# Fewer idle products before the experts, and the expert probabilities moved into the first expert

## The chip, the cores and the metric

The kernel runs on one core of a Trainium2 chip. The metric is the device time of one execution in microseconds (us). The engines of the core work side by side, each through its own list of instructions in order: TensorE (PE in the rows; its weight loads are PEld), VectorE (DVE), ScalarE (ACT), GpSimd (POOL) and SyncE (SP, which here mainly starts transfers). They wait for each other by semaphores.

## The reference

Three stages follow each other, on 2 x 768 tokens of 384 numbers (8 heads of 48):

```python
# 1 attention: a state that is updated token by token
y[:, :, t] = np.einsum('bhd,bhde->bhe', q[:, :, t], state)
v_old = np.einsum('bhde,bhd->bhe', state, kt)
state = state + bt[:, :, :, None] * np.einsum('bhd,bhe->bhde', kt, vt - v_old)
# 2 experts: one of 8 for each token, kept from the token before if local_gate >= 0.5
fresh_e = int(np.argmax(logits[b, s]))
e = fresh_e if s == 0 or local_gate[b, s] < 0.5 else (prev_e if prev_e >= 0 else fresh_e)
p = np.exp(logits[b, s] - logits[b, s].max()); p /= p.sum() + 1e-09
out[b, s] = p[e] * (np.maximum(x[b, s] @ w1[e], 0.0) @ w2[e])
# 3 mixing: FFT over tokens and features, a norm, and one more MLP
u = x + mixed
ch = np.maximum(un @ w_ch1, 0.0) @ w_ch2
out = u + ch
```

Each expert has weights of 384 x 1024 and 1024 x 384. The probability `p[e]` scales an expert's output, so it is needed only when the first expert's output is written; which expert a token goes to is needed before the first product.

## The kernel before

**Stages.** Attention ends at about 240 us of the profiled execution, the routing at about 257, the experts at about 390; the mixing takes the rest. Attention is ordered by a planner (not touched here). From the routing on, the order on each engine is that of the code, with one exception: between the routing and the experts stands a branch (L989, L990) for tokens that overflow an expert's 240 slots. With these inputs its body is not entered, but all five engines read the flag and go past it. When the program is built, an instruction written behind the branch may be put ahead of it where nothing that it needs is made in between.

**Routing** (`route`, L734 to L812) turns the logits `lg` into lists. On VectorE a chain of small instructions (from `mx`, L750) finds each token's expert (`e`, as one-hot `Ot`), its rank among the expert's tokens (`rank`), and one-hots of the slot (`oh`, L801). Twelve products on TensorE (`st`) then give the list of token numbers per slot. Behind them stand the idle products: `warm(s.WARMR)`, L806, multiplies a constant by itself into the PSUM tile `wp` (L746) 20 times, and nothing reads it. In the trace each appears as two instructions. From `st` VectorE makes the gather's indices `gm` and the overflow flag `fl`. GpSimd then gathers expert 0's tokens into `xg` (L901, two indirect transfers) and, behind the branch, expert 1's. The logits minus their maximum are kept in `ls`.

**Weights.** Each expert has 4 weight pairs (a block of w1 and one of w2), 32 in all, loaded by SP into six buffers `raw` (`wload`, L855, two transfers a pair). Each number is split into a high and a low fp16 part: `whi` (L891) makes the high part on ScalarE, `wlo` (L894) the low part on VectorE from `raw` and the high part. `wlo(q)` also issues the loads of pair q+6. `whi(0)` and `whi(1)` are called ahead of the routing, `whi(2)` and `whi(3)` behind it.

**Experts** (`moe_main`, L943). First come `chosen` (L817 to L829: one exponential on ScalarE, L820, then 11 VectorE instructions that make the probability `pr` and its three fp16 parts `pp`), `wlo(0)`, and the transposes of expert 0's tokens: `xtr` transposes a third of the features on TensorE (`xtp`, L907), ScalarE copies the high part (L908), VectorE makes the low part (L909). For expert 0 the three thirds have three buffers; for later experts the tile `t` has one. Then, for each weight pair q: `h` makes 18 products (`hp`, L918), ScalarE the high part of their relu (`hh`, L920), VectorE the low part (`hl`, L921); a third of the next expert's tokens is transposed; `o` makes 12 products with the pair before (`op`, L930). In expert 0 there is more: `parts` (L813 to L816) multiplies `pp` into the one-hots, part 1 at pair 1, parts 2 and 3 at pair 2, and `slots_p` (L830 to L836) makes, at pair 3, the probability of each slot with 12 products that read `oh` and the result of `parts` (L834). Its PSUM tile is `t` too, the one buffer that the transposes use.

Of the kernel before, what the change touches and what calls it, by code (L numbers as in the profile page):

```python
# [728 lines left out]
class Rest:  # L729
    def __init__(s,tc,I,O,K,xd,x2d):  # L730
        s.tc,s.nc,s.I,s.O,s.K,s.xd,s.x2d=tc,tc.nc,I,O,K,xd,x2d

    WARMR=20
    def route(s,keep,pool,ps,lg):  # L734

        nc,K=s.nc,s.K; V,G=nc.vector,nc.gpsimd
# [8 lines left out]
        def warm(n):  # L745
            for _ in range(n): nc.tensor.matmul(out=wp,lhsT=K["ident"],rhs=K["ident"],start=True,stop=True)  # L746
# [58 lines left out]
        for j in range(12): nc.tensor.matmul(out=st,lhsT=oh[:,j],rhs=s.Wr[:,0,:,j],start=(j==0),stop=(j==11))  # L805
        warm(s.WARMR)  # L806
        s.gi=s.gidx(keep,st.rearrange("p h e -> p (h e)"),16,"m")
# [134 lines left out]
        s.scattered.append(i)  # L942
    def moe_main(s):  # L943
        dec=s.decoding(); s.sc=[]; s.scattered=[]; last=None
        s.chosen()
        s.wlo(0)
        for k in range(3): s.xtr(0,k,"h",3)
        s.wlo(1)
        next(dec)
        for q in range(32):  # L950
            e,g=divmod(q,4)
            if g==0 and e<7: s.gather(e+1)
            x=s.h(q)
            if g and e<7: s.xtr(e+1,g-1)
            s.whi(q+4)
            if last: s.o(q-1,last)
            last=x
            if q==0: s.wlo(2)
            s.wlo(q+3)
            if q==1: s.parts(1)  # L960
            if q==2: s.parts(2); s.parts(3)
            if q==3: s.slots_p()
            if g==1:
                while s.sc: s.scatter()
            if q==26: s.tables(0)
            if q==29: s.tables(1)
            if q>2:
                for _ in range(1+(g==0)): next(dec,None)
        for t in range(2):
            s.o(31,last,(t,))  # L970
            while s.sc: s.scatter()
        p=s.ps.tile([128,2,256],F32,tag="h",name="wp",bufs=3)
        for _ in range(s.WARMM): s.nc.tensor.matmul(out=p[:,0,0:128],lhsT=s.K["ident"],rhs=s.K["ident"],start=True,stop=True)

        z=s.wk.tile([128,2],F32,name="z")
        s.nc.gpsimd.memset(z[:,0:1],0.0)
        s.nc.vector.tensor_copy(out=z[:,1:2],in_=z[:,0:1])
        for _ in dec: pass
        s.wlo(35)
        for q in (36,37):  # L980
            s.whi(q); s.wlo(q)
# [546 lines left out]
```

## Time and profile before

| | |
|---|---|
| median of 3 runs | 582.86 us (581.4 to 585.84) |
| profiled execution | 580.74 us, of which the span of the trace 578.9 us |
| granted TensorE clock, mean over the span | 0.909 |
| TensorE busy | 470.7 us (81% of the span), 5162 instructions |
| VectorE busy | 421.7 us (73%), 943 |
| ScalarE busy | 322.8 us (56%), 729 |
| GpSimd busy | 78.9 us (14%), 85 |

The trace is of one execution, and its times are microseconds from the start of its span. A share of busy time is a mean over stages that have different limits, so the rows below are read by stretch: what each engine does there, and for whom it waits. The clock stands as a fraction of full speed: 1.00 is the level of 2.4 GHz, 0.50 that of 1.2 GHz.

### The profile page before, as it was taken

Reading aid. Unit: us, or ns where it says so; the run is one execution under the profiler, and the core shown is the slowest. Engines: PE = TensorE matmul, PEld = TensorE weight load, DVE = VectorE, ACT = ScalarE, POOL = GpSimd, SP = SyncE. Lnnn points to the kernel's source line nnn. Section 1 sums busy time; section 2 is a strip of 40 time slices with the busy share of each in tenths; the row PEclk is TensorE's granted clock in tenths of the full one; section 3 lists DMA queues with packets and bytes.
Section 4 is the critical chain, followed back from the end, with each engine's and each line's share of the span. In section 5 each row is a group of like instructions: output and inputs, shape, how many; then the busy total and the mean of one; then the engine's idle time right before and its main releaser. Section 6 shows DMA issues by size and latency. Waiting matters only on the chain.

```text
span 578.9 us, 12899 instructions
## 1 busy us (share of the span) xinstructions
PE 470.7 (81%) x5162; PEld 375.0 (65%) x5162; DVE 421.7 (73%) x943; ACT 322.8 (56%) x729; POOL 78.9 (14%) x85
## 2 busy tenths in 40 slices
PE   0642027894689799679999999999899999999997
PEld 0531017783689698568888888788787655555575
DVE  7969989898998877469888979878987643231132
ACT  3664347898698888716766766672554332111111
POOL 6000000000000000040343332125111210000010
PEclk9965556999599789879999999999999999999999
DMA  7274125186005103839999997328100000010011
GB/s 250 50 130 121 37 49 63 63 141 156 1 3 103 29 3 100 299 99 336 388 319 316 361 305 238 118 63 274 56 1 1 28 2 0 1 55 0 1 42 41
DMA packets 66991, 67.23 MB, mean 116 GB/s; under 512 B 40086, under 2 KB 59483, under 8 KB 66928
## 3 DMA queue, kind: packets, MB, share of 16 engines
q1 hardware_dynamic: 63936, 57.59, 33.5%
q0 software_dynamic: 2992, 8.79, 4.9%
q8 instruction: 41, 0.67, 0.5%
q14 instruction: 22, 0.18, 0.1%
HBM read 51.95 MB, written 7.67 MB: 103 GB/s over the span
## 4 chain that ended last, share of the span: by engine, by line
PE 27%; issue 18%; POOL 5%; DVE 3%; DMA 1%; ACT 1%; POOLq 0%; SPq 0%; ACTq 0%; DVEq 0%
PE mp L1373 12%; PE mop L1399 12%; POOL xg L901 3%; POOL x2d L939 2%; PE fp L1239 1%; PE yp L1208 1%; DMA xa<-x2d 1%; PE up L1320 1%; DVE zl L1192 0%; DMA x2d<-ot,sim 0%; ACT zh L1190 0%; DVE e L1127 0%; DVE Y L1265 0%; DVE ws L894 0%; DVE d L1127 0%
## 5 line engine op out<-in xcount | busy, mean ns | idle before, releaser
L1383 DVE SCALAR_TENSOR_TENSOR ml<-mp,mh 128x256 f16<-128x256 f32 (+1 forms) x48 | 26.8, 558 | 81.0 <-ACT mh L1381 80.9
L1373 PE MATMUL mp<-uT,ws 128*128 128x256 f16 (+1 forms) x432 | 77.8, 326 | 0.0
L1399 PE MATMUL mop<-ws,mh 128*128 128x384 f16 x288 | 77.7, 326 | 0.0
L1381 ACT ACTIVATE mh<-mp 128x256 f16<-128x256 f32 (+1 forms) x48 | 23.5, 489 | 89.8 <-PE mp L1373 89.6
L930 PE MATMUL op<-ws,hh 128*128 128x384 f16 (+1 forms) x256 | 67.5, 326 | 0.0
L918 PE MATMUL hp<-xT,ws 128*128 128x240 f16 x576 | 64.6, 266 | 0.9 <-DVE xT L909 0.5
L312 PEld LDWEIGHTS <-KT 128*128 128x128 f16 x576 | 27.5, 118 | 51.6 <-issue 40.1
L918 PEld LDWEIGHTS <-ws 128*128 128x128 f16 x576 | 56.2, 98 | 6.9 <-issue 1.3
L1373 PEld LDWEIGHTS <-ws 128*128 128x128 f16 x432 | 42.2, 98 | 27.2
L894 DVE SCALAR_TENSOR_TENSOR ws<-raw,ws 128x1536 f16<-128x1536 f32 x32 | 55.9, 1749 | 0.0
L312 PE MATMUL ga<-ST,KT 128*128 128x64 f16 x288 | 16.2, 224 | 42.2 <-DVE ST L308 37.7
L891 ACT ACTIVATE ws<-raw 128x1536 f16<-128x1536 f32 x32 | 47.3, 1485 | 0.7 <-DMA raw<-moe_w 0.7
L1399 PE MATMUL mop<-ws,ml 128*128 128x384 f16 x144 | 46.9, 326 | 0.0
L930 PE MATMUL op<-ws,hl 128*112 128x384 f16 (+1 forms) x128 | 41.7, 326 | 0.0
L1399 PEld LDWEIGHTS <-mh 128*128 128x128 f16 x288 | 28.2, 98 | 17.8
L901 POOL DMA_INDIRECT xg<-xd,gm x16 | 23.0, 1437 | 117.4 <-DVE fl L1063 110.0
L930 PEld LDWEIGHTS <-hh 128*128 128x128 f16 (+1 forms) x256 | 29.1, 114 | 11.6
L373 DVE TENSOR_TENSOR P<-P,tmp 128x31 f32<-128x31 f32 (+15 forms) x93 | 31.5, 338 | 1.7
L371 DVE TENSOR_TENSOR tmp<-Gu,P 128x31 f32<-128x31 f32 (+15 forms) x93 | 31.2, 336 | 1.6
L921 DVE SCALAR_TENSOR_TENSOR hl<-hp,hh 128x480 f16<-128x480 f32 x32 | 20.9, 654 | 14.5 <-ACT hh L920 12.9
L939 POOL DMA_INDIRECT x2d<-ot,sim x16 | 19.3, 1204 | 86.9 <-ACT ot L935 84.4
L920 ACT ACTIVATE hh<-hp 128x480 f16<-128x480 f32 x32 | 18.1, 567 | 20.7 <-PE hp L918 19.5
(274 smaller groups left out, 1176.9 us busy)
## 6 DMA issues: line engine op xcount, KB each, us to landing
raw<-moe_w SPq DMA_DIRECT2D x64, 384.0 KB
x<-moe_w_ch SPq DMA_DIRECT2D x24, 384.0 KB
qp<-q SPq DMA_DIRECT2D x5, 512.0 KB
kp<-k SPq DMA_DIRECT2D x6, 384.0 KB
vp<-v SPq DMA_DIRECT2D x6, 384.0 KB
xd<-yb SPq DMA_DIRECT2D x48, 48.0 KB
xa<-x2d SPq DMA_DIRECT2D x6, 384.0 KB
ur<-x2d SPq DMA_DIRECT2D x2, 768.0 KB
```

The costliest lines, as they stand in the source:

```text
L312: s.nc.tensor.matmul(out=out,lhsT=st[l],rhs=mv[m],start=(first and i==0),stop=True,skip_group_check=True)
L371: nc.vector.tensor_tensor(out=x,in0=Gu[:,k,k+1:32].unsqueeze(2).to_broadcast([128,m,n]),in1=P[:,k,0:n].unsqueeze(1).to_broadcast([128,m,n] ...
L373: nc.vector.tensor_tensor(out=P[:,k+1:32,0:n],in0=P[:,k+1:32,0:n],in1=x,op=ALU.subtract)
L891: s.nc.scalar.activation(out=s.W[q][:,0].rearrange("p s c -> p (s c)"),in_=s.raw[q],func=AF.Copy,scale=WS)
L894: s.nc.vector.scalar_tensor_tensor(out=W[1],in0=s.raw[q],scalar=WS,in1=W[0],op0=ALU.mult,op1=ALU.subtract)
L901: nc.gpsimd.indirect_dma_start(out=s.xg[e][t][0:w],out_offset=None,in_=s.xd,in_offset=bass.IndirectOffsetOnAxis(ap=s.gi[0:w,8*t+e:8*t+e+1] ...
L918: nc.tensor.matmul(out=p[:,i],lhsT=s.W[q][:,a,i,128*k:128*k+128],rhs=xT[b][:,k],start=(n==0),stop=(n==8)); n+=1
L930: nc.tensor.matmul(out=s.po[t][0:w],lhsT=hs[a][:,i,128*t:128*t+w],rhs=s.W[q][:,b,i,384:768],start=(g==0 and i==0 and n==0),stop=(g==3 and ...
L939: i=s.nc.gpsimd.indirect_dma_start(out=s.x2d,out_offset=bass.IndirectOffsetOnAxis(ap=s.si[0:w,c:c+1],axis=0),in_=ot,in_offset=None,bounds_ ...
L1373: for k in range(3): nc.tensor.matmul(out=p,lhsT=s.w_ch1(a,k,f),rhs=s.uT[g][b][:,k,0:N],start=(n==0),stop=(n==8)); n+=1
L1383: nc.vector.scalar_tensor_tensor(out=hl,in0=p,scalar=0.0,in1=hh,op0=ALU.max,op1=ALU.subtract)
L1399: nc.tensor.matmul(out=pm[t],lhsT=hs[a][:,128*t:128*t+128],rhs=s.w_ch2(b,f),start=(f==0 and n==0),stop=(f==11 and n==2))
```

## The change

There are three edits. The number of idle products goes from 20 to 13. `chosen()` is no longer called at the head of `moe_main`, so that `wlo(0)` is the first call there. And `chosen()` is called at weight pair 1 instead, just ahead of `parts(1)`. (The overflow branch has a call of its own to `chosen`, which stays.) Behind L945 the lines of the changed kernel have numbers that are lower by one.

```diff
-    WARMR=20
+    WARMR=13
     def route(s,keep,pool,ps,lg):
...
         dec=s.decoding(); s.sc=[]; s.scattered=[]; last=None
-        s.chosen()
         s.wlo(0)
         for k in range(3): s.xtr(0,k,"h",3)
...
             s.wlo(q+3)
-            if q==1: s.parts(1)
+            if q==1: s.chosen(); s.parts(1)
             if q==2: s.parts(2); s.parts(3)
             if q==3: s.slots_p()
```

On VectorE, at the start of the routing (the copies of the logits `lg` end attention, `mx` begins the routing), the built program differs by one row:

```order
L540 SCALAR_TENSOR_TENSOR U_116<-ups,U_113 64x96 x2
L643 COPY lg<-eps 32x9 x3
+L894 SCALAR_TENSOR_TENSOR ws<-raw,ws 128x1536
L750 TENSOR_REDUCE mx<-lg 128x12
L752 SCALAR_TENSOR_TENSOR rf<-lg,rc 128x12
```

The low part of weight pair 0 is still written behind the branch, where `chosen` stood ahead of it, but with `chosen` gone it is built ahead of the whole routing.

SyncE's list at the same place, with the last writes of attention's output (`xd`), the overflow flag (`fl`), and the weights' loads (`raw`), before:

```order
L855 DMA raw<-moe_w 128x2x384 x12
L160 DMA xd<-yb 32x4x96 x8
L989 TENSOR_LOAD fl
```

and after:

```order
L855 DMA raw<-moe_w 128x2x384 x12
L160 DMA xd<-yb 32x4x96 x8
L855 DMA raw<-moe_w 128x2x384 x2
L988 TENSOR_LOAD fl
```

The two loads of pair 6, which `wlo(0)` issues, moved with it to the place ahead of the flag.

On ScalarE, the first instructions behind the branch, with the semaphores for which each waits in brackets (`ex` is the exponential in `chosen`, `xT` the transposed tokens of expert 0), before:

```order
L820 ACT_TABLE_LOAD [waits DVE_49]
L820 ACTIVATE ex<-ls 128x96 [waits Activation_49]
L908 ACTIVATE xT<-xtp 128x240 [waits DVE_49,DMASW6_49,PE_49,Activation_49]
L908 ACTIVATE xT<-xtp 128x240 [waits PE_49] x2
L920 ACTIVATE hh<-hp 128x480 [waits PE_49]
```

and after:

```order
L908 ACT_TABLE_LOAD [waits DVE_49,DMASW6_49,PE_49]
L908 ACTIVATE xT<-xtp 128x240 [waits Activation_49]
L908 ACTIVATE xT<-xtp 128x240 [waits PE_49] x2
L920 ACTIVATE hh<-hp 128x480 [waits PE_49]
L891 ACTIVATE ws<-raw 128x1536 [waits DMAHW7_49,DMAHW6_49,Pool_49]
L920 ACTIVATE hh<-hp 128x480 [waits PE_49]
L908 ACTIVATE xT<-xtp 128x240 [waits PE_49]
L891 ACTIVATE ws<-raw 128x1536 [waits DMAHW1_49,DMAHW0_49]
L820 ACTIVATE ex<-ls 128x96
```

The table load now belongs to the first copy of transposed tokens, and stands behind that copy's wait for TensorE; the exponential follows eight rows later.

On VectorE in expert 0, from the low part made at pair 1 on, before:

```order
L894 SCALAR_TENSOR_TENSOR ws<-raw,ws 128x1536
L815 TENSOR_TENSOR ph<-pp,hi 128x24
L816 TENSOR_TENSOR W<-Ot,ph 128x96 x2
L921 SCALAR_TENSOR_TENSOR hl<-hp,hh 128x480
L909 SCALAR_TENSOR_TENSOR xT<-xtp,xT 128x240
```

and after, down to the first row of `parts`:

```order
L894 SCALAR_TENSOR_TENSOR ws<-raw,ws 128x1536
L821 TENSOR_REDUCE se<-ex 128x12
L822 TENSOR_TENSOR t_4385<-Ot,ex 128x96
L823 TENSOR_SCALAR se<-se 128x12
L824 TENSOR_REDUCE pr<-t_4385 128x12
L825 RECIPROCAL se<-se 128x12
L826 TENSOR_TENSOR pr<-pr,se 128x12
L828 CAST pp<-pr 128x12
L829 TENSOR_TENSOR pr<-pr,pp 128x12
L828 CAST pp<-pr 128x12
L829 TENSOR_TENSOR pr<-pr,pp 128x12
L828 CAST pp<-pr 128x12
```

The eleven instructions of `chosen` stand between the low part and `parts(1)`; the rows behind them are the same as before.

## Rows read from the trace of the kernel before

**Rows 1.** Windows by stage: busy time of each engine, clock, DMA share, GB/s:

```profile
core 0: us, PE busy (x) PEld busy (x) DVE busy (x) ACT busy (x) POOL busy (x), PEclk, DMA share, GB/s
240.80:249.70 8.90, 2.45 (x28) 1.69 (x29) 6.95 (x31) 4.50 (x4) 0.00 (x0) 0.51 0.41 133
249.70:256.80 7.10, 7.04 (x43) 6.85 (x43) 3.83 (x17) 1.57 (x2) 3.86 (x4) 0.66 0.39 108
262.60:272.90 10.30, 10.30 (x82) 8.30 (x80) 10.20 (x20) 6.44 (x9) 0.00 (x0) 1.00 1.00 354
272.90:390.00 117.10, 116.88 (x940) 97.34 (x939) 100.30 (x116) 79.70 (x106) 36.60 (x29) 1.00 0.78 267
```

**Rows 2.** Grouped lines, TensorE, 262.6 to 390 us: busy, mean ns, idle before:

```profile
L918 PE MATMUL hp<-xT,ws 128*128 128x240 f16 x543 | 61.0, 266 | 0.2
```

**Rows 3.** Timeline, start of the routing: start, us, engine, line, operation [idle before]:

```profile
239.70 1.48 ACT L891 ACTIVATE ws<-raw 128x1536 f16<-128x1536 f32 x1
...
240.61 0.17 DVE L643 COPY lg<-eps 32x9 f32<-32x9 f32 x1 [0.61 <-PE eps L637]
240.82 0.25 DVE L750 TENSOR_REDUCE mx<-lg 128x12 f32<-128x96 f32 x1
```

**Rows 4.** Timeline from the idle products to the first transposes:

```profile
249.75 6.99 PE L746 MATMUL wp<-ca 128*128 128x128 f32 x40
...
250.39 1.03 POOL L901 DMA_INDIRECT xg<-xd,gm  x1 [110.04 <-DVE fl L1063]
...
251.72 0.94 POOL L901 DMA_INDIRECT xg<-xd,gm  x1 [0.30 <-POOLq L990]
251.82 1.28 ACT L820 ACT_TABLE_LOAD   x1 [6.52 <-DVEq L990]
...
253.12 0.28 ACT L820 ACTIVATE ex<-ls 128x96 f32<-128x96 f32 x1
253.43 0.25 DVE L821 TENSOR_REDUCE se<-ex 128x12 f32<-128x96 f32 x1 [2.77 <-issue]
...
254.22 0.94 POOL L901 DMA_INDIRECT xg<-xd,gm  x1 [0.30 <-DMA xg<-xd,gm]
...
255.48 1.76 DVE L894 SCALAR_TENSOR_TENSOR ws<-raw,ws 128x1536 f16<-128x1536 f32 x1
257.22 0.62 PEld L907 LDWEIGHTS xtp<-ca,xg 128*128 128x128 f32 x6 [0.67 <-PEq L990]
257.25 0.82 PE L907 MATMUL xtp<-ca,xg 128*128 128x128 f32 x6 [0.51 <-DVE ws L894]
```

**Rows 5.** DMA issues, 253.5 to 255 us: the gather's, and us to landing:

```profile
xg<-xd,gm POOLq DMA_INDIRECT x2, 3.1
```

**Rows 6.** Timeline, expert 0: TensorE and the ScalarE row used:

```profile
264.81 2.01 PE L918 MATMUL hp<-xT,ws 128*128 128x240 f16 x18
...
266.86 0.57 ACT L920 ACTIVATE hh<-hp 128x480 f16<-128x480 f32 x1 [1.80 <-PE hp L918]
...
268.81 2.01 PE L918 MATMUL hp<-xT,ws 128*128 128x240 f16 x18
...
272.90 0.46 PE L834 MATMUL sp<-W,oh 128*128 128x48 f16 x12
...
273.20 0.47 PE L918 MATMUL hp<-xT,ws 128*128 128x240 f16 x3
```

**Rows 7.** Timeline, expert 0: VectorE:

```profile
266.03 1.75 DVE L894 SCALAR_TENSOR_TENSOR ws<-raw,ws 128x1536 f16<-128x1536 f32 x1
...
267.70 0.17 DVE L815 TENSOR_TENSOR ph<-pp,hi 128x24 f16<-128x24 f16 x1
...
268.24 0.65 DVE L921 SCALAR_TENSOR_TENSOR hl<-hp,hh 128x480 f16<-128x480 f32 x1
...
272.44 0.40 DVE L909 SCALAR_TENSOR_TENSOR xT<-xtp,xT 128x240 f16<-128x240 f32 x1
```

**Rows 8.** Windows of half a microsecond around the clock's rise:

```profile
254.50:255.00 0.50, 0.50 (x6) 0.50 (x5) 0.42 (x3) 0.00 (x0) 0.50 (x1) 0.96 0.71 138
```

## The prediction

> **What bounds the kernel now.** I read the windows by stage first [rows 1]. From 262.6 us to 390 us TensorE is busy for 10.30 of 10.30 us and 116.88 of 117.10 us: the experts are bound by it, and the grouped lines put only 0.2 us of idle time before its products there [rows 2]. So a delay at the experts' first product, or a stall inside expert 0, reaches the end of the kernel in full. The 18 us ahead of that (240.8 to 258.6) are the routing: a chain of small VectorE instructions, with TensorE busy for 2.45 of 8.90 us and then only with idle products. This stretch is all that the change touches, with expert 0.
>
> The timeline of the routing's start [rows 3] shows VectorE copying the last logits at 240.61 and starting the routing's first reduction at 240.82, with no gap. ScalarE begins the first of four high parts at 239.70 and needs 1.48 us for it.
>
> The timeline from the idle products to the first expert [rows 4] shows three things. The idle products run from 249.75 for 6.99 us, to 256.74; the first transposes follow at 257.25, 0.51 us later. The gather's data are there earlier: the first gather starts at 250.39, and the fourth, which waits for its landing, starts at 254.22, 3.8 us after; the second starts at 251.72 and lands 3.1 us (the fourth gather's landing time, [rows 5]) to 3.8 us later, at 254.8 to 255.5. And the probabilities (table load at 251.82, VectorE from 253.43) and weight pair 0's low part (255.48 to 257.24) run beside the idle products. All this is covered by the idle products, and the transposes wait for their end alone: the row names the low part (its end, 257.24) as what released them, but their weight load began at 257.22, before it.
>
> In expert 0, VectorE is busy for 10.20 of 10.30 us [rows 1]. TensorE there moves in lockstep: one product group starts at 264.81 and the next at 268.81, 4.00 us; the one after starts at 273.20, 4.39 us later [rows 6]. Between them are the 12 slot products, 0.30 us (272.90 to 273.20), so 0.09 us was waiting. What they waited for is VectorE: its third low part of the next expert's tokens runs 272.44 to 272.84 [rows 7], reads the PSUM tile `t` of which there is one buffer, and the slot products need that buffer; they start at 272.90. VectorE's slack there is nothing.
>
> **The change, part by part.** *The low part of pair 0 moves, and further than its line says.* The order of the built program puts it, with its two weight loads on SP's queue, ahead of the routing's first reduction. It needs the high part, done at 239.70 + 1.48 = 241.2, and takes 1.76 us [rows 4]: to 242.9. The reduction, at 240.82 before, starts 2.1 us later, and with it the whole routing, the idle products (251.85), the gathers and the branch: all on VectorE's chain or behind it. SP's two loads stand behind the last writes of attention and in front of SP's read of the overflow flag; they wait for 242.9, the flag is due at 252. Their 0.79 MB fall into the routing, whose DMA share is 0.41 [rows 1], and cost nothing; were they late, they would meet the gathers at 252.5.
>
> *13 idle products in place of 20.* Each is two instructions, so 26 in place of 40. TensorE's clock stood at half (0.51 on the mean, the 1.2 GHz level) through the routing [rows 1] and rose to full by 254.5, 4.8 us after the first idle product (0.96 in 254.5 to 255.0) [rows 8]. With 4.75 us at half and 2.24 us at full clock for 40, one takes (4.75 + 2 x 2.24) / 40 = 0.23 us at half and 0.115 at full. If the clock rises at the same moment, 254.5, 2.65 us at half clock do 11.5 of the 26 and the other 14.5 take 1.67 us: the end is 256.2. If it rises only 4.8 us after the later start, at 256.65, 20.9 are done by then and the end is 257.25. So the end lies between 256.2 and 257.3 (256.74 before), and the transposes could start at 256.7 to 257.8. The second gather lands at 254.8 + 2.1 = 256.9 at the earliest, 257.6 at the latest. The pair of transposes for the first third ends at about 257.25 with the early bounds (before: 257.25 + 0.4 = 257.65), a gain of 0.4 us; with the late ones at 258.2, a loss of 0.55. I take the early bounds, because the fourth gather belongs to the same burst and the clock's rise is read at 254.5: **-0.4 us** (range -0.4 to +0.55). The 7 products that go pay for 2.1 us of later routing, and no more.
>
> *ScalarE's table load.* Before, the first ScalarE instruction behind the branch was the exponential, so its table load, 1.28 us at 251.82, lay beside the idle products. In the built order the load now stands at the copy of the first transposed tokens, and the wait for TensorE stands on the load, not behind it. ScalarE takes its instructions in order, so the load starts when the transposes end: **+1.28 us** on the path to the first product. It costs nothing only if it could be run ahead of its wait, and the exponential at 253.12, 0.01 us behind the load's end, shows nothing more than 1.28 either: bounds 0 and 1.28, and I take the row. The Trainium skill (ScalarE: Activation LUTs, What ACT_TABLE_LOAD costs) gives 1283 ns for the load and some 1380 ns of drain more. The trace agrees on the first and shows no drain, ScalarE having stood idle before; an estimate from the page's two figures makes the sum 4.3 us, not 2.9.
>
> *The probabilities go into expert 0.* Eleven small VectorE instructions ran from 253.43 until the low part started at 255.48: **2.05 us**. They now stand behind the low part of 266.03 and in front of the part at 267.70 [rows 7]. Everything behind them on VectorE, up to the tokens' low part that ends at 272.84, has no gap, so it comes 2.05 us later, and TensorE's slot products with it: +2.05 in full. Bounds: 0, if VectorE could catch up; 2.05 by the rows. The exponential (0.28) goes into ScalarE's idle 1.80 us ahead of 266.86 [rows 6] and costs nothing. Behind the slot products both engines are late by the same amount.
>
> **Sum:** -0.4 + 1.28 + 2.05 = +2.9 us. The profiled execution took 580.74 us (span 578.9), so 583.7 for it. The three timed runs have their median at 582.86, 2.1 us above the profiled one, and spread from 581.4 to 585.84; on that median the forecast is 582.86 + 2.9 = 585.8 us, 0.5% slower. About 1% is what a measurement of this kernel can tell from no change, so this lies within it.
>
> **Rivals.** *The late bounds hold* (clock and landing): +0.55 in place of -0.4, +3.9 us, 586.8. For it speaks that nothing ties the clock's rise to a time in the program; against it, the 254.5 in the rows. Chance 0.17.
>
> *The table load is hidden*: -0.4 + 2.05 = +1.65, 584.5. Against it stands the order of the waits. Chance 0.10. *It costs twice its row*, a wait as long again behind it: +1.28 more, 587.1. The exponential began 0.01 us behind the load's end, so 0.03. The Trainium skill (ScalarE: Activation LUTs, What ACT_TABLE_LOAD costs) names such a wait.
>
> *Not slower: VectorE catches up in expert 0.* If the slot products do not wait, as they would not with 2.05 us of idle time on VectorE ahead of 272.4, the sum is +0.9, 583.7, no difference. It decides at slack 2.05 us; the rows show 0.1. Chance 0.10. Coming out over 1% faster would need this, a hidden load and more.
>
> *Slower by over 1%: the idle products end before the clock rises*, and it stays at half into expert 0. Twenty products rose it after 4.8 us; 13 last 26 x 0.23 = 6.0 us at half clock, so 1.2 us decide. If it fails, the transposes start at 251.85 + 6.0 + 0.5 = 258.35, 1.1 later than before, and the first 4.8 us of expert products run at half speed and lose 2.4: 1.1 + 0.2 (transposes) + 1.28 + 2.4 + 2.05 = +7.0, 589.9. Chance 0.06. The Trainium skill (TensorE: Matmul & The Clock Gate, What's actually happening) says that the slow state is the default and activity lifts it; by that, the cut idle products are the risk of this change.
>
> *The weights arrive earlier.* Pair 6's load starts some 13 us sooner; but products waited 0.2 us in all behind 262.6 [rows 2], so at most 0.2 is gained, and it is left out.
>
> **How the numbers follow.** Forecast with its own terms 0.50 (585.8), late bounds 0.17 (586.8), hidden load 0.10 (584.5), costlier load 0.03 (587.1), caught up 0.10 (583.7), cold clock 0.06 (589.9), anything else 0.04. The range leaves out the cold clock and takes in the others, with some of the spread of the runs: from caught up and hidden load together (582.86 - 0.4 = 582.5, and 0.5 of spread: 582.0) to the costlier load (587.1, and 1.1 of spread: 588.2). Slower than 588.7 (over 1%): the cold clock and the spread above the late bounds, 0.10. Faster than 577.0: 0.03. Within 1%: 0.87.
>
> **What would show each step.** Right: the routing's reduction near 242.9, behind a low part; a table load just behind the first transposes, with the experts' first product near 259.5 (258.60 before); the slot products near 272.90 + 0.9 + 2.05 = 275.8; TensorE without gaps behind. Wrong: a reduction still at 240.8; a load that ended before the transposes; slot products that come only as late as the first product; or a granted clock of 0.50 behind 258.

## The result, and the profile after

| | before | changed |
|---|---|---|
| median of 11 runs each | 583.06 us | 588.13 us (587.01 to 590.3) |
| ratio, 95% interval | 1 | 1.0089 (1.0072 to 1.0106) |
| profiled execution | 580.74, span 578.9 | 588.09, span 586.3 |
| mean granted clock | 0.909 | 0.895 |

The changed kernel is slower by 5.2 us (583.06 x 0.0089; 4.2 to 6.2 by the interval). The forecast was +2.9 us and 585.8; the measured 588.13 lies at the very top of its range. Direction and most of the places were right, the size was not: 2.3 us were missing.

The two spans differ by 7.4 us, more than the medians, and the first reading is why. Rows of the timeline at the start of the routing, after (start, us, engine, line, operation, idle time before):

```profile
242.68 0.17 DVE L643 COPY lg<-eps 32x9 f32<-32x9 f32 x1 [0.61 <-PE eps L637]
243.28 1.76 DVE L894 SCALAR_TENSOR_TENSOR ws<-raw,ws 128x1536 f16<-128x1536 f32 x1 [0.43 <-ACT ws L891]
244.96 0.24 DVE L750 TENSOR_REDUCE mx<-lg 128x12 f32<-128x96 f32 x1
```

Attention ended 2.07 us later in this execution (last logits at 242.68; 240.61 in [rows 3]), with nothing of the change in it. In the 17 traces of this study the last logits lie between 240.6 and 244.7, in four executions of the changed kernel alone between 242.3 and 242.7. So where times of two traces are compared below, each is counted from the last logits of its own trace. Counted so, the reduction `mx` starts at 2.28, before at 0.21: the low part ahead of the routing costs 2.07 us, as forecast (2.1).

What follows on TensorE and ScalarE up to the first product, after, in the same view (rows [rows 4] answer to these):

```profile
253.88 5.89 PE L746 MATMUL wp<-ca 128*128 128x128 f32 x26
...
260.23 0.82 PE L907 MATMUL xtp<-ca,xg 128*128 128x128 f32 x6 [0.45 <-PE wp L746]
260.70 1.28 ACT L908 ACT_TABLE_LOAD   x1 [13.33 <-PE xtp L907]
...
262.00 0.89 ACT L908 ACTIVATE xT<-xtp 128x240 f16<-128x240 f32 x3
...
262.86 5.51 PE L918 MATMUL hp<-xT,ws 128*128 128x240 f16 x36 [1.81 <-DVE xT L909]
```

The 13 idle products, 26 instructions in the trace, take 5.89 us, 0.227 us an instruction: nearly as long as the 40 instructions of before (6.99). The table load stands alone between the transposes and the copies, and TensorE waits 1.81 us behind the transposes, where it was 0.53 before. And the 36 products of the first two groups take 5.51 us; before, two rows of 19 and 17 took 2.11 and 1.92:

```profile
258.60 2.11 PE L918 MATMUL hp<-xT,ws 128*128 128x240 f16 x19 [0.53 <-DVE xT L909]
260.90 1.92 PE L918 MATMUL hp<-xT,ws 128*128 128x240 f16 x17 [0.19 <-DVE ws L894]
```

The windows say why (busy time, clock, DMA share and GB/s of a stretch): the idle products, the transposes and the wait, the first two groups, and the experts behind expert 0's stall:

```profile
core 0: us, PE busy (x) PEld busy (x) DVE busy (x) ACT busy (x) POOL busy (x), PEclk, DMA share, GB/s
253.90:259.70 5.80, 5.80 (x29) 5.58 (x28) 0.67 (x5) 0.00 (x0) 3.85 (x4) 0.50 0.38 104
260.20:262.80 2.60, 0.82 (x6) 0.69 (x7) 0.40 (x2) 2.09 (x4) 1.27 (x2) 1.00 0.13 45
262.90:268.10 5.20, 5.20 (x35) 4.29 (x35) 3.45 (x5) 1.85 (x2) 0.51 (x1) 0.67 0.57 163
...
280.80:390.00 109.20, 108.95 (x874) 90.32 (x870) 94.99 (x110) 72.38 (x98) 34.03 (x26) 1.00 0.80 269
```

The granted clock is 0.50 (1.2 GHz) through all the idle products, 1.00 (2.4 GHz) through the transposes and the wait, in which TensorE was busy for 0.82 of 2.60 us, and 0.67 on the mean over the first two groups. Before, the idle products had 0.66 on the mean [rows 1], and the same two groups had 1.00:

```profile
258.60:262.60 4.00, 3.81 (x36) 3.39 (x36) 3.60 (x5) 1.97 (x3) 2.74 (x2) 1.00 0.75 256
```

Behind 280.8 TensorE is busy for 108.95 of 109.20 us, so nothing ahead is given back there.

In expert 0, after (VectorE, and the two places where TensorE waits for it):

```profile
273.31 0.25 DVE L821 TENSOR_REDUCE se<-ex 128x12 f32<-128x96 f32 x1
...
275.20 0.17 DVE L828 CAST pp<-pr 128x12 f16<-128x12 f32 x1
275.28 0.16 DVE L815 TENSOR_TENSOR ph<-pp,hi 128x24 f16<-128x24 f16 x1
...
276.84 0.43 PE L907 MATMUL xtp<-ca,xg 128*128 128x128 f32 x2 [0.46 <-DVE xT L909]
...
280.02 0.40 DVE L909 SCALAR_TENSOR_TENSOR xT<-xtp,xT 128x240 f16<-128x240 f32 x1
...
280.48 0.46 PE L834 MATMUL sp<-W,oh 128*128 128x48 f16 x12 [1.25 <-DVE xT L909]
```

The probabilities take 1.97 us of VectorE (273.31 to 275.28). Behind them TensorE waits twice for a low part of the tokens that has to leave the one buffer `t`: 0.46 us at the third transpose, 1.25 us at the slot products. The waits of TensorE from 253 us on name the same places:

```profile
engine line waited for: us in total, times, longest us
PE hp L918 <- DVE xT L909: 1.8, 1, 1.8
PE sp L834 <- DVE xT L909: 1.3, 1, 1.3
...
PE xtp L907 <- DVE xT L909: 0.5, 1, 0.5
```

### The profile page after: what moved, and what is told of

The parts are those of the page before. It is cut to its first block, busy times and chain, and to the rows that moved or that the text cites. A ratio compares the mean times of both kernels' runs of the same rounds, so it can differ in the third digit from the quotient of the medians.

```text
span 586.3 us, 12869 instructions
## 1 busy us (share of the span) xinstructions
PE 472.8 (81%) x5148; PEld 376.2 (64%) x5148; DVE 421.7 (72%) x943; ACT 322.5 (55%) x729; POOL 77.1 (13%) x85
## 4 chain that ended last, share of the span: by engine, by line
PE 36%; issue 21%; DVE 21%; ACT 9%; DMA 7%; POOL 5%; SPq 1%; POOLq 0%; ACTq 0%; DVEq 0%
PE mp L1372 12%; PE mop L1398 12%; POOL xg L901 3%; DVE P L373 3%; DVE tmp L371 3%; DMA raw<-moe_w 2%; DMA KT<-KBl 2%; POOL x2d L939 2%; PE wps L312 2%; PE fp L1238 1%; ACT U L512 1%; DMA vp<-v 1%; PE lps L614 1%; PE yp L1207 1%; PE wp L746 1%
## 5 line engine op out<-in xcount | busy, mean ns | idle before, releaser
L918 PE MATMUL hp<-xT,ws 128*128 128x240 f16 x576 | 66.1, 270 | 2.1 <-DVE xT L909 1.8
L930 PE MATMUL op<-ws,hh 128*128 128x384 f16 (+1 forms) x256 | 67.5, 326 | 0.0
L918 PEld LDWEIGHTS <-ws 128*128 128x128 f16 x576 | 57.2, 99 | 8.5 <-issue 2.6
L930 PE MATMUL op<-ws,hl 128*112 128x384 f16 (+1 forms) x128 | 41.7, 326 | 0.0
L930 PEld LDWEIGHTS <-hh 128*128 128x128 f16 (+1 forms) x256 | 29.1, 114 | 11.6
L901 POOL DMA_INDIRECT xg<-xd,gm x16 | 20.8, 1302 | 118.2 <-DVE fl L1062 112.0
```

Source lines behind the costliest of these rows:

```text
L901: nc.gpsimd.indirect_dma_start(out=s.xg[e][t][0:w],out_offset=None,in_=s.xd,in_offset=bass.IndirectOffsetOnAxis(ap=s.gi[0:w,8*t+e:8*t+e+1] ...
L918: nc.tensor.matmul(out=p[:,i],lhsT=s.W[q][:,a,i,128*k:128*k+128],rhs=xT[b][:,k],start=(n==0),stop=(n==8)); n+=1
L930: nc.tensor.matmul(out=s.po[t][0:w],lhsT=hs[a][:,i,128*t:128*t+w],rhs=s.W[q][:,b,i,384:768],start=(g==0 and i==0 and n==0),stop=(g==3 and ...
```

## The experiments

The times of a kernel are given as its ratio to the kernel before, timed on the same chip, with the 95% interval, and in us of 583. Lines inserted in a kernel shift the numbers behind them.

**13 idle products alone.** The kernel before with one edit:

```diff
-    WARMR=20
+    WARMR=13
```

> The kernel before with 13 idle products in place of 20, and nothing else. In the changed kernel all 26 instructions of the idle products ran at half clock, 0.2265 us each. From 249.75 us on, where they start in the kernel before, that ends at 255.65 in place of 256.74, so the transposes and the experts' first product come 1.1 us earlier. Theory 1 (the clock is what 13 products cost): the clock then stands at half in part of expert 0's first two product groups, which cost 1.3 us in the changed kernel, so the time is about that of before: +0.2 us, 583.3 (from -1.1 to +0.6). Rival (the half clock there was a chance of that one execution): -1.1 us, 582.0.

Measured: 0.9989 (0.9971 to 1.0006), -0.6 us (-1.7 to +0.3). Its timeline on TensorE:

```profile
251.94 4.72 PE L746 MATMUL wp<-ca 128*128 128x128 f32 x26
257.33 0.30 PE L907 MATMUL xtp<-ca,xg 128*128 128x128 f32 x1 [0.68 <-DVE pr L829]
258.48 0.73 PE L907 MATMUL xtp<-ca,xg 112*128 112x112 f32 x5 [0.84 <-DMA xg<-xd,gm]
259.79 2.11 PE L918 MATMUL hp<-xT,ws 128*128 128x240 f16 x19 [0.58 <-ACT xT L908]
```

The same 26 instructions took 4.72 us here, 5.89 in the changed kernel: the clock rose 3.3 us after the first of them, there only behind the last. The transposes start 2.2 us earlier than before, but half of that is lost at once, since the second transpose waits 0.84 us for the second gather, issued at 253.90; the wait ends 4.6 us behind the issue. The first product comes 1.1 us earlier, at full clock. The time lies between the two expectations; it decides neither, but 13 products as such cost nothing.

**The move alone, with 20 idle products.** The changed kernel with `WARMR=20`:

> The changed kernel with the 20 idle products of before: only the move of the probabilities and of the first low part is left. Theory 1: routing 2.06 us later, idle products as long as before (6.99 us), so the transposes 2.06 later; the table load 1.28; the stall in expert 0 2.0; no product of expert 0 at half clock, less 0.2 for a wait that goes: +5.1 us, 588.2, the same as the changed kernel. Rival (the half clock in expert 0 has nothing to do with the number of idle products): the changed kernel's +5.1 and another 1.15 for the longer idle products: +6.2 us, 589.3.

Measured: 1.0086 (1.0059 to 1.0114), +5.0 us. In its trace the first product comes 3.8 us later than before and the slot products 5.8 us later, with the clock at 1.00 from the transposes on. The time fits theory 1; the interval (3.4 to 6.6) holds the rival's 6.2 too, and the trace lies between the two. So the idle products taken away gain nothing in the changed kernel that can be measured.

**The low part kept behind the branch.** The changed kernel with a VectorE instruction that stays behind the branch, since the branch's body writes the same tile:

```diff
         dec=s.decoding(); s.sc=[]; s.scattered=[]; last=None
+        s.nc.vector.memset(s.se,0.0)
         s.wlo(0)
```

> The changed kernel with one VectorE instruction more (a memset of 128x12 that nobody needs) ahead of the first low part, which keeps the low part behind the branch, where it was before. Theory 1 (the low part ahead of the routing costs its whole 2.06 us): -2.06 us against the changed kernel, +3.0 against before, 586.1; the table load (1.28) and the stall in expert 0 (2.0) stay. With the clock as in the changed kernel 585.9 to 586.3; with full clock in expert 0 1.3 us less. Rival (the routing's start is not on the path, the gain is lost on the gather or on the clock): no difference to the changed kernel, 588.1.

Measured: 1.0048 (1.0024 to 1.0072), +2.8 us, against +5.2 for the changed kernel: 2.4 us for the place of the low part. The routing starts at 0.21 again. The kernel before with its **two first calls exchanged** is the other side of this, nothing but the low part ahead:

```diff
-        s.chosen()
         s.wlo(0)
+        s.chosen()
```

> The kernel before with the two first calls of the experts exchanged: the first low part, then the probabilities; 20 idle products. As in the changed kernel the built program has the low part ahead of the routing, but the probabilities and their table load stay beside the idle products, and expert 0 is as before. Theory 1 (the four terms are separate): the routing 2.06 us later and nothing else, the gather landing well before the idle products' end: +2.1 us against before, 585.4 (to +2.6 if the clock rises as late as in the run with the probabilities moved and 20 idle products, where those took 7.52 us in place of 6.99). Rival (the low part ahead of the routing is worth something later, by pair 6's earlier loads): under +1, 584.

Measured: 1.0039 (1.002 to 1.0059), +2.3 us. Two kernels that differ from their partners by this place alone give 2.4 us (some 0.7 to 4.1) and 2.3 us (1.2 to 3.4), and the routing's start moves by 2.07 in the traces: the term is there, and no gain by pair 6's earlier loads shows beside it. Part of the 2.4 can be the clock, which did not fall in the trace of the first kernel and did in three traces of the changed one (below).

The kernel with the calls exchanged and that with the move and 20 idle products differ in nothing but the place of the probabilities: +2.3 against +5.0, so 2.7 us (some 0.7 to 4.7), and 3.2 us at the slot products in their traces (34.90 and 38.09 us after the last logits). That is the table load and the stall in expert 0 together, forecast at 1.28 + 2.05 = 3.3 us.

**The table load covered again.** The changed kernel with the exponential alone at the head of the experts, the rest of the probabilities still at pair 1:

```diff
         dec=s.decoding(); s.sc=[]; s.scattered=[]; last=None
+        s.nc.scalar.activation(out=s.ex,in_=s.ls,func=AF.Exp)
         s.wlo(0)
...
-            if q==1: s.chosen(); s.parts(1)
+            if q==1: s.chosen(False); s.parts(1)
```

(`chosen(False)` leaves out its exponential.)

> The changed kernel with the exponential alone put back to the head of the experts, ahead of the copies of the transposed tokens, so that the table load runs beside the idle products; the 11 VectorE instructions stay in expert 0. Theory 1 (the load behind its wait costs 1.28 us): -1.28 us against the changed kernel, +3.8 against before, 586.9. Rival (a load costs more than its row, by a wait behind it as long again): -2.5 us, 585.6. Rival (the load is hidden): no difference, 588.1.

Measured: 1.0038 (1.002 to 1.0056), +2.2 us. ScalarE in its trace:

```profile
256.01 1.28 ACT L945 ACT_TABLE_LOAD   x1 [8.58 <-DVEq L990]
257.31 0.28 ACT L945 ACTIVATE ex<-ls 128x96 f32<-128x96 f32 x1
260.87 0.90 ACT L908 ACTIVATE xT<-xtp 128x240 f16<-128x240 f32 x3 [3.28 <-issue]
```

The load lies beside the idle products, and the first product follows the transposes after 1.48 us in place of 2.63. By the trace the load is worth 1.2 us; the medians differ by 3.0 us (each known to about 1). The clock can make up part of the rest: in this trace it stayed at 1.00 through the first two groups.

**The changed kernel again, three times.** Since one trace was the ground for the clock:

> The changed kernel once more, for a second trace: how long its 26 idle products take, whether TensorE's clock falls again in expert 0, and where the milestones stand against the last logits. Theory 1 (the half clock in expert 0 comes from the idle stretch of 2.6 us between the idle products and the first expert product and falls in some executions): either 5.5 us from the last logits to the end of the slot products above those of before, with a granted clock of 0.5 in part of expert 0, or 4.2 with full clock. Rival (attention is slower in the changed kernel, by the 2.07 us by which it ended later in its first trace): the last logits again at 242.7, where the other runs have 241.8 to 243.6.

> The changed kernel a third time, for a third trace. In the first the 26 idle products took 5.89 us, all at half clock, and the clock fell again for 3.4 us in expert 0; in the second they took 5.21 us and it did not fall. Theory 1: the end of the slot products against the last logits is 4 to 5.5 us above that of before (32.6), 1.28 us of it behind the transposes by the table load and 2.0 in expert 0 by VectorE; what differs between the three is the clock and the landing of the second gather (3.1 to 4.5 us).

> The changed kernel timed again, on one chip with the next, for a fourth trace. In two of its three traces the clock fell for 3.4 us in expert 0 and the first output product came 1.6 us later for it. Theory 1: +5.2 us against before, 588.3.

Measured: single times of 586.96 and 588.35, and for the last 1.0072 (1.0046 to 1.0098), +4.2 us. The four traces of the changed kernel beside that of before, in us from the last logits, each read from the rows of its timeline as above:

| | before | first | second | third | fourth |
|---|---|---|---|---|---|
| first idle product | 9.14 | 11.20 | 11.20 | 11.19 | 11.20 |
| end of the idle products | 16.13 | 17.09 | 16.41 | 16.96 | 16.75 |
| first transpose | 16.64 | 17.55 | 16.87 | 17.41 | 17.19 |
| first product (L918) | 17.99 | 20.18 | 19.91 | 20.30 | 20.37 |
| first output product (L930) | 22.25 | 25.74 | 24.16 | 25.75 | 25.56 |
| slot products (L834) | 32.29 | 37.80 | 36.18 | 38.12 | 37.94 |
| later than before | | 5.51 | 3.89 | 5.83 | 5.65 |
| mean clock, first product to first output product | 1.00 | 0.69 | 1.00 | 0.70 | 0.74 |

The mean of "later than before" is 5.22, which is the measured +5.2. So close a match is partly luck: there is one trace of before, and its 40 instructions of idle products took 6.99 us, where those of the two other kernels with 20 idle products took 7.52 and 7.61. In three of the four the clock fell again, at 0.7 us ahead of the first product at the earliest and 0.5 us behind it at the latest; the second has no fall and reaches the slot products 1.6 to 1.9 us sooner than the others. Its windows over the idle products and the first two groups:

```profile
253.60:258.70 5.10, 5.10 (x29) 4.94 (x26) 0.67 (x5) 0.00 (x0) 3.63 (x4) 0.58 0.36 92
262.30:266.20 3.90, 3.71 (x36) 3.29 (x36) 3.49 (x5) 1.94 (x2) 0.47 (x1) 1.00 0.46 97
```

Here the clock rose 0.9 us ahead of the end of the idle products (0.58 on their mean) and stayed.

**The wait filled.** The changed kernel with four idle products where TensorE waited for the table load:

```diff
         for k in range(3): s.xtr(0,k,"h",3)
+        p=s.ps.tile([128,384],F32,tag="o",name="wf",bufs=4)
+        for _ in range(4): s.nc.tensor.matmul(out=p[:,0:128],lhsT=s.K["ident"],rhs=s.K["ident"],start=True,stop=True)
```

> The changed kernel with 4 idle products more (8 instructions, 0.9 us at full and 1.8 us at half clock) between the transposes and the experts' first product, where TensorE waited 2.2 us for the table load and the copies. Theory 1 (TensorE's idle stretch lets the clock fall in expert 0 in some executions, which costs 1.3 us there): the first product is not later, the clock stays at full through expert 0, and the median lies 0.3 to 1.3 us under that of the changed kernel (+5.2 against before): +4.4, 587.5. Rival (the clock fell by chance and seldom): no difference, +5.2.

> The changed kernel with 4 idle products more between the transposes and the experts' first product, timed again beside the changed kernel. Theory 1 (the idle stretch there lets the clock fall, which costs 1.3 us in two of three executions): no fall in the trace, and 0.6 to 1.4 us under the changed kernel of the same chip. Rival (the fall has nothing to do with that stretch): no difference, within 0.4 us.

Measured: 1.0064 (1.0046 to 1.0082), and 1.0081 (1.0053 to 1.0109) beside the changed kernel's 1.0072 on the same chip. In the first of the two traces, TensorE:

```profile
260.84 1.07 PE L948 MATMUL wf<-ca 128*128 128x128 f32 x8
262.81 2.11 PE L918 MATMUL hp<-xT,ws 128*128 128x240 f16 x19 [0.91 <-DVE xT L909]
```

and its window over the first two groups:

```profile
262.90:266.80 3.90, 3.71 (x36) 3.29 (x36) 3.49 (x5) 1.94 (x2) 0.46 (x1) 1.00 0.39 95
```

In both traces the clock stayed at 1.00, the first product was not later, and the slot products came 36.35 and 36.39 after the last logits, 1.6 us sooner on the mean than in the three traces with a fall. The times do not confirm it: 1.5 us under the changed kernel's first +5.2, but 0.5 over it where both were timed on one chip. Over all 17 traces the clock fell again in 3 of the 6 in which TensorE waited 1.8 us ahead of the first product, and in 1 of the 11 others.

The two filled traces do not tell the filling from chance, since the clock rose early in both. In the four traces with a fall it had risen 0.5 us ahead of the end of the idle products or later (in the first trace of the changed kernel 0.1 us behind it), and TensorE then stood idle for 1.8 to 2.6 us in all before the first product. In the filled traces it had risen 1.7 and 0.9 us ahead, and TensorE still stood idle for 2.5 and 1.8 us, since it waited for the second gather and the table load too. In the second trace of the changed kernel it had risen 0.9 us ahead as well; that one did not fall with nothing filled in, and had its slot products at 36.18. What speaks for the wait are other traces: with the exponential at the head, and with idle products spread over the routing (below), the clock rose as late (0.15 and 0.4 us ahead), TensorE stood idle for 1.0 and 1.2 us only, and the clock stayed. So the falls came where a late rise met a long wait. That is read from 17 traces afterwards, and no run tests it.

**Idle products spread over the routing.** The kernel before with 13 at their place and 8 more in the routing (`warm(2)`, `warm(1)`, `warm(1)`, `warm(4)` ahead of the products of L760, L771, L783 and L805; the first two ran just ahead of the last logits, the others in the routing's waits):

> The kernel before with 21 idle products in another distribution: 13 at their old place, and 2, 1, 1 and 4 more in the stretches of the routing in which TensorE waits for VectorE. Theory 1 (the clock rises after some time of activity of TensorE, and a late rise is what makes 13 products long): the clock is at full before or soon after the last 13 begin, these take 2.9 to 4.0 us in place of 6.99, and the transposes wait for the gather's second landing alone, 14.1 to 15.5 us after the last logits (the two landings seen so far) in place of 16.6 for the transposes: -1.1 to -2.5 us against before, 581.6. Rival (the idle products of the gaps stand in front of the routing's own products, at half clock 0.45 us each): the routing is later by up to 1 us, and the time is that of the run with 13 idle products alone, 583. Second rival on the gather: in all four traces with 13 idle products the second gather took 4.4 to 4.5 us to land and 16 KB of instructions were loaded meanwhile, in both with 20 it took 3.0 and none were; here then 4.4 again.

Measured: 1.0016 (0.9995 to 1.0037), +0.9 us. A miss. The windows over a part of the routing with spread products in it, and over the last 13:

```profile
246.70:250.30 3.60, 3.14 (x23) 2.52 (x22) 2.36 (x11) 2.19 (x2) 0.00 (x0) 0.50 0.15 36
...
253.45:259.05 5.60, 5.60 (x29) 5.45 (x27) 2.42 (x15) 1.57 (x2) 3.86 (x4) 0.53 0.39 103
```

TensorE was busy for 3.14 of 3.60 us and the clock stayed at 0.50; it rose 14.5 us after the last logits (13.9 in the next kernel, which has the spread products too), and between 12.3 and 13.9 in the six traces with the same routing and none of them. More activity earlier did not bring the rise forward. **The same with the first low part ahead of the probabilities**, behind the branch:

> The same with the first low part ahead of the probabilities but behind the branch (a memset of 128x12 that nobody needs stands in front of it and keeps it there). Theory 1: where the gather lands early, the experts' first products would wait for the low part, which ends 16.6 us after the last logits in the kernel before; ahead of the probabilities it ends some 2 us sooner: 0 to -0.8 us against the run with distributed idle products, 581.2. Rival (the probabilities are then late for the tokens' low part): +0.3 to +1 us against it.

Measured: 0.9995 (0.9973 to 1.0018), 1.2 us under the kernel it is compared with, though the two first products stand at 16.90 and 17.08: the traces show 0.2 of it, and the two intervals, over 2 us each, overlap.

**16 and 10 idle products**, both with that order of low part and probabilities:

> The kernel before with 16 idle products, and the first low part ahead of the probabilities but behind the branch (a memset of 128x12 that nobody needs keeps it there). In all runs so far a load of 16 KB of instructions begins 3.5 to 3.7 us after the first of 13 idle products and 7.1 to 7.2 us after the first of 20, 0.5 us per product; with 13 it lies upon the second gather, whose landing took 4.4 to 4.5 us in six traces and 3.1 in one, with 20 it lies behind and the landing took 3.0 to 3.1. Theory 2 (that load delays the gather): with 16 it begins 5.1 us after the first, 3.1 after the second gather's issue; the gather lands after 3.0 us, the transposes wait for the idle products alone: -0.5 to -1.5 us against before, 582.2. Rival (the gather is slow for another reason): 4.4 again.

> The same with 10 idle products. They end 4.5 us after their first (half clock), 13.6 us after the last logits in place of 16.1. Theory 2: the load of instructions begins 2.0 us after the first idle product, with the second gather's issue; whether it delays the gather from there no run has shown: the first product 1.1 us (landing after 4.5 us) to 2.5 us (3.0) earlier than before, 580.7 to 582.1 by that. Theory 1 on the clock: with 2.3 us less of activity it rises later or falls again, and expert 0's first products cost 1.3 to 2.4 us more: 582 to 584 in sum. Rival (the clock rises at the same moment all the same): 580.7.

Measured: 0.9989 (0.9971 to 1.0008) and 0.9986 (0.9968 to 1.0004). With 16 the second gather landed after 3.2 us, and the first product came at 16.91, 1.1 us earlier than before, as expected; the interval of the time (-1.7 to +0.5 us) holds that, and no difference too. With 10 the gather landed after 3.8 us. There, TensorE:

```profile
255.23 1.16 PE L907 MATMUL xtp<-ca,xg 128*128 128x128 f32 x6 [1.11 <-DMA xg<-xd,gm]
256.92 5.51 PE L918 MATMUL hp<-xT,ws 128*128 128x240 f16 x36 [0.53 <-DVE xT L909]
```

and the window of the first two groups:

```profile
256.95:262.20 5.25, 5.25 (x36) 4.26 (x36) 3.18 (x5) 1.57 (x3) 2.71 (x2) 0.67 0.87 264
```

The first product came 1.9 us earlier than before (16.11), then the two groups took 5.51 us at a mean clock of 0.67, and the slot products were 0.2 us earlier only: the fall took most of the gain back, 1.3 of 1.9 us, without any table load in the way.

**The best of it.** The kernel before with 12 idle products, that order, and one idle product between the transposes and the first product:

```diff
-    WARMR=20
+    WARMR=12
...
-        s.chosen()
+        s.nc.vector.memset(s.se,0.0)
         s.wlo(0)
+        s.chosen()
         for k in range(3): s.xtr(0,k,"h",3)
+        p=s.ps.tile([128,384],F32,tag="o",name="wf",bufs=4)
+        s.nc.tensor.matmul(out=p[:,0:128],lhsT=s.K["ident"],rhs=s.K["ident"],start=True,stop=True)
```

> The kernel before with 12 idle products, the first low part ahead of the probabilities but behind the branch, and one idle product more between the transposes and the experts' first product. With 10 idle products and none there the first product came 1.9 us earlier than before, but the clock fell in expert 0 and took 1.3 us back. Theory 1: with TensorE active in the gap the clock stays, the first product comes 1.1 to 2.0 us earlier than before and all of it reaches the end: 581.4 to 582.3. Rival (the clock falls all the same): -0.7 us, 582.7, as with 10.

Measured: 0.9976 (0.9952 to 1.0000), -1.4 us, 581.47. Its trace has the clock at 1.00 behind the first product, and the marks about 1.5 us ahead of before: first product 16.45, slot products 30.74. Its ratio is the lowest here, about 1% under the changed kernel's (1.0089 and 1.0072); against the kernel before its interval ends at no difference, and it overlaps those with 10, 13 and 16 idle products. Whether the one product in the wait kept the clock is not shown: with 13 idle products alone the clock stayed without it.

## Why the prediction came out too low

| step | forecast | mean of the four traces |
|---|---|---|
| start of the transposes | -0.4 (-0.4 to +0.55) | +0.62 (0.23 to 0.91) |
| transposes to first product | +1.28 | +1.59 (1.28 to 1.83) |
| first two product groups | 0 | +0.85 (-0.01 to 1.30) |
| expert 0 up to the slot products | +2.05 | +2.17 (1.98 to 2.34) |
| sum | +2.9 | +5.2 |

**The step that failed is the clock's rise**, in the term for the start of the transposes: -0.4 us was forecast, +0.62 measured. "4.8 us after the first idle product", and the moment 254.5, were read from one trace [rows 8], and the early bound took the moment as given. In the 17 traces here the rise comes between 2.8 and 6.1 us after the first idle product of the last batch. In the first trace of the changed kernel it came at 6.0 us, behind the last of the 26 instructions. The right upper bound was already in the text, in the rival on the cold clock: 13 products at half clock need 6.0 us and end 1.1 us later than before. It stood there with a chance of 0.06, as if it needed a failure; it needs only a late rise. That is 1.0 of the missing 2.3 us.

**The clock's fall in expert 0** was in the rivals as a clock that does not rise at all. What happened lies between: it rose, and fell to half again for part of the first two product groups, in three of four executions, which cost 0.9 to 1.3 us each time and 0.85 on the mean. The sum had nothing for it. The Trainium skill (TensorE: Matmul & The Clock Gate, What's actually happening) says that the throttled state is the default and that activity lifts it. The traces agree: the clock stood at 0.50 through most of the routing and rose 4.3 to 6.0 us after the first idle product of the changed kernel. That the cut in idle products is a risk was drawn from it rightly; that TensorE's waits behind them may be part of the risk, and that the table load lengthens these, was not considered.

**The table load** was right: 1.28 us on the path, behind the wait, in every trace of the changed kernel. The page named in the prediction (the Trainium skill, ScalarE: Activation LUTs, What ACT_TABLE_LOAD costs) would add a drain of 1.38 us; the load ended at 261.98 and the copy began at 262.00, so the trace shows none, here where ScalarE had waited for TensorE. The 0.3 us more in the mean are the second gather: in three of the four traces the transposes that need it came 0.26, 0.41 and 0.55 us late. The late bound on the gather was the truer one, and still too early: 3.8 us to the landing there, 4.5 and 4.6 in the two of these traces that have the landing on record (below).

**The probabilities in expert 0** were right, in place and size: VectorE had no slack, and TensorE's two waits (0.46 and 1.25 us) sum to most of the 2.0 us.

**The routing's delay** was right (2.07), and the sentence that 7 fewer products pay for it was too kind: by the mean above they pay for some 1.4 of the 2.07 us.

What stays open is how often the clock falls, and by what. The traces have it in three of four, and the two comparisons of the filled wait with the unfilled one do not agree. And the 2.07 us by which attention ended later in the first trace are not shown to belong to the change: the other 13 traces have their last logits anywhere from 240.6 to 244.7.

## What to carry to other kernels

In both kernels here the first ScalarE instruction behind the branch brought a table load of 1.28 us, and in the changed one that load took over the instruction's wait: let one stand there whose inputs are ready long before the critical path comes by. Work that becomes the first behind a branch may be built ahead of it, as the low part was, into another critical chain, so read the built order and not the source. And where a price hangs on the moment at which a clock rises, one trace is one draw (2.8 to 6.1 us here): bound the stretch by all of it at half clock, and look at the waits behind it as well.

## What the runs showed of the hardware

**The second gather landed later in the traces in which instructions were loaded meanwhile.** In each trace a packet of 16 KB on a queue for instructions starts at nearly the same time after the first of the last idle products: 3.5 to 3.8 us with 12 or 13 of them, 2.4 with 10, 4.8 with 16, 7.0 to 7.2 with 20. Neither the first trace of the changed kernel nor that of before has the landing of its second gather on record. From its issue on the queues moved, after, in the 4.37 us up to the first transposes (packets, MB, share of 16 engines):

```profile
q0 software_dynamic: 204, 0.63, 52.4%
q14 instruction: 4, 0.03, 3.2%
q8 instruction: 1, 0.02, 2.0%
```

and before, in the first 3.01 us:

```profile
q0 software_dynamic: 131, 0.38, 47.4%
q14 instruction: 4, 0.03, 4.5%
```

The packet on q8 is there after, where it begins 1.6 us behind the issue, and not before, where it begins 5.2 us behind it. The issue row of that one gather, with the us to its landing, in the fourth trace of the changed kernel:

```profile
xg<-xd,gm POOLq DMA_INDIRECT x1, 4.6
```

and with 16 idle products, where the packet begins 2.9 us after the issue:

```profile
xg<-xd,gm POOLq DMA_INDIRECT x1, 3.2
```

In the traces whose landings are all on record it is 4.3 to 4.6 us in four with 13 products, 4.0 with 12, 3.8 with 10 and 3.2 with 16. The "3.0 to 3.1" for 20, and the one "3.1" for 13 that the expectations name, come from traces that lack some landings; in the latter TensorE stopped ahead of the transpose that reads the gather until 4.2 us after the issue, so it looks like no exception. The Trainium skill (Runtime: NRT & Kernel Launch, Instruction fetch mechanics) says that instructions are refilled in blocks of 16 KiB, and that a taken branch out of the loaded part forces a refill; the size agrees with the packet, and which engine loads here no row says. That the load delays the gather rests on this order of times, with one trace each for 16, 12 and 10; it was not tried by itself, and the first gather of the four traces with 13 takes anything from 3.5 to 4.4 us to land. What the rows do show is that the number of idle products ahead of this branch sets when the packet starts.
